# A one-core state-space convolution and MLP kernel: one polar form computed with logarithms and exponentials, table products on POOL, one scratch pool, a new order

## The chip, the cores and the metric

The kernel runs on one core of one Trainium2 chip. A core has five engines with queues of their own: TensorE (PE in the profile, its weight loads PEld), VectorE (DVE), ScalarE (ACT), GpSimd (POOL) and SyncE (SP, which here only issues DMAs). The metric is the device time of one execution in microseconds, lower is better; each kernel is run several times and the median counts.

## What is computed

The reference takes u (1 x 2048 x 512, bfloat16) and computes a state-space convolution with a residual, and then an MLP with a residual:

```python
dt = jnp.exp(log_dt)[:, None]
logdA = dt * (A_re + 1j * A_im)                       # D=512 x N=128
P = jnp.exp(logdA[:, :, None] * l[None, None, :])     # l = 0..L-1, L=2048
K = jnp.einsum("dn,dnl,dn->dl", Cc, P, dt * Bc).real
y = irfft(rfft(pad(u_n)) * rfft(pad(K)))[:L] + u_n * Dskip   # u_n = layernorm(x)
h = x + y
h2 = h + (gelu(layernorm(h) @ w1 + b1) @ w2 + b2)     # 512 -> 1376 -> 512
```

## The kernel before

The program has a front (parameters, tables, first transform, generation of the convolution kernel), a middle (the rest of the transforms and the products in frequency space) and the MLP. The 512 channels are done in two halves of 256 (numbers 0 and 1 in the names below).

*Parameters* (`params`). The coefficient of each state is dt times B times C, a complex number g = (gr, g_i), held as 512 columns on 128 partitions. It is taken to polar form: |g| by a square root, the angle by an arctangent of a half-angle quotient, with a sign s (plus or minus one half) from gr. Tiles w0 to w5 of the pool "w" hold these. The magnitude becomes `amp`; the angle is added to the phase `pc`. The phases are cut into bf16 pieces in `src_p` and `src_q` (parts of M), which TensorE turns into `lps`, and these are copied to PQ0 and PQ1.

*Tables* (`outer`). RP (128 x 1024) and RQ (128 x 640) are outer products of small tables of counts, wp and wq, and of a folded identity m. TensorE multiplies PQ by RP or RQ into `pv` and `qv`, which are phases for all of the powers needed; ScalarE takes their sines (`s`, `sq`).

*Powers.* exp(dt A l) is split into 32 coarse powers (Pt) and 20 fine ones (Q). ScalarE writes the magnitudes with Exp (`exps`), VectorE multiplies Q by amp, and then both by the sines (`p_half`, `q_half`). Each half has 8 products on Pt (of two instructions) and 10 on Q.

*Kernel generation* (`kgen`, L718). For each half, TensorE multiplies Q and Pt in four groups of 256 small matmuls, `kps`; ScalarE copies one part of each to `ku`, VectorE combines both into `samples`. These go to memory (KD_near, KD_far) and come back turned, as `kt`. Groups one and two need the first quarter of the channels, three and four the second.

*First transform* (`norm_in`, L791 to L807). After bn_stats and the roots of the layer norm, sixteen rows of u are normalised (`u`, two buffers), multiplied on TensorE by BD (`aps`), cast to bf16 (`a`, four buffers) and stored by SP to A_dram. Four loads of 1 MB each bring A_dram back as X (L819). `xps` is the next step of that transform, cast into X again.

*Transform tables* (`tables`). M holds the matrices of the transforms, made from sines; the parts `M<-base,Dp` are products of `base` and of `Dp`, which POOL loads out of Dd (L415) after SP has written `ds` there (L400). `R` is copied out of the transposes `rps`.

*Middle* (`conv`). `kfps` is the spectrum of the kernel (from kt), `zps` the first step of the way back; z goes to memory as Zd and comes back turned as ZT, from which TensorE makes the rows `y` and `yh`.

PSUM has three slots "p" that nearly all these tiles share, and one "q".

*The order.* Nothing here is scheduled at run time. Each step is registered as an operation of a list, with the engine or engines that may take it, its rough cost, and the steps it needs. `S.run(ORDER)` then issues the operations in the order of a table of numbers: a number divided by four names the operation, and the rest says which of its engines takes it. Engines then run their queues in that order, and wait on semaphores where an input or a buffer isn't ready.

*Activation tables.* ScalarE's functions lie in sets, and a load (ACT_TABLE_LOAD) stands where the next function isn't in the one that is loaded. In the front before there are loads at the start, for Sqrt (L562), for Sin (L122) and for the second half's Exp (L632).

## Time and profile before

| | before |
|---|---|
| median of 3 runs | 280.96 us |
| lowest, highest | 279.72, 285.02 us |
| the profiled execution's time | 281.15 us |
| its span, first to last instruction | 279.4 us |
| mean granted TensorE clock in the span | 0.901 |
| busy: TensorE, VectorE, ScalarE, POOL | 238.2, 212.5, 173.5, 36.8 us |
| DMA traffic | 31.88 MB, mean 114 GB/s |

The span lies inside the time of the execution; 1.75 us are outside it. Times in the rows are microseconds from the start of the span. A row of the timeline has start, duration, engine, line, operation, output and inputs, a count where rows are put together, and in brackets how long the engine was idle before and what ended that. "issue" stands where the profile shows nothing that was waited for. Rows of one engine overlap by about 0.1 us, so the pace of a chain is taken from start to start.

### The profile page before, as it was taken

How to read it: one execution, taken by the hardware profiler on the slowest of the kernel's cores; microseconds unless marked ns; L12 is line 12 of the kernel's file. 1: busy time of each engine (PE TensorE's matmuls, PEld its weight loads, DVE VectorE, ACT ScalarE, POOL GpSimd, SP SyncE). 2: the span in 40 equal slices, each digit the busy share in tenths (PEclk: the TensorE clock that was granted, in tenths of full speed). 3: DMA queues.
4: the chain of work that ended last, by engine and by line, in shares of the span. 5: the costliest groups of instructions: out<-in, count | busy, mean ns of one | idle time of the engine just before them, and what ended most of it. 6: DMA issues, size and time to landing. Idle time of an engine off the chain costs nothing.

```text
span 279.4 us, 6128 instructions
## 1 busy us (share of the span) xinstructions
PE 238.2 (85%) x2419; PEld 154.9 (55%) x2434; DVE 212.5 (76%) x439; ACT 173.5 (62%) x288; POOL 36.8 (13%) x97
## 2 busy tenths in 40 slices
...
DVE  4999999999973999999669899975672682682012
ACT  4999999999876999997042435215850640630720
...
GB/s 169 263 3 0 38 153 38 158 274 146 124 329 54 146 105 0 37 114 6 5 157 170 236 195 237 264 168 82 322 76 87 31 20 101 33 19 109 25 19 56
DMA packets 41912, 31.88 MB, mean 114 GB/s; under 512 B 14506, under 2 KB 40348, under 8 KB 41628
## 3 DMA queue, kind: packets, MB, share of 16 engines
...
q8 instruction: 19, 0.31, 0.5%
...
## 4 chain that ended last, share of the span: by engine, by line
PE 62%; DVE 19%; ACT 8%; issue 5%; DMA 5%; SPq 0%; DVEq 0%; ACTq 0%; POOLq 0%
PE h1ps L1160 14%; PE o2ps L1172 13%; PE kfps L882 10%; PE kps L718 7%; DVE X L86 4%; DVE st L782 3%; ACT sq L122 3%; PE qv L689 2%; DVE w L74 2%; DMA Zd<-z 1%; DMA ZT<-Zd 1%; DVE Pt L74 1%; PE pv L655 1%; PE y L1119 1%; PE aps L798 1%
## 5 line engine op out<-in xcount | busy, mean ns | idle before, releaser
L1162 ACT ACTIVATE hT<-h1ps,b_sb 128x512 bf16<-128x512 f32 (+3 forms) x55 | 32.4, 601 | 41.2 <-PE h1ps L1160 41.1
L1160 PE MATMUL h1ps<-y2T,wide 128*128 128x512 bf16 (+3 forms) x217 | 40.6, 340 | 0.1
L882 PE MATMUL kfps<-kt,M 128*128 128x256 bf16 x320 | 39.2, 273 | 0.0
L1172 PE MATMUL o2ps<-w_sb,hT 128*128 128x512 bf16 (+3 forms) x183 | 38.5, 366 | 0.2
L74 DVE TENSOR_TENSOR ot<-o2ps,h 128x512 bf16<-128x512 f32 (+1 forms) x17 | 11.0, 658 | 31.1 <-PE o2ps L1172 19.9
L882 PEld LDWEIGHTS <-M 128*128 128x128 bf16 x320 | 31.3, 98 | 5.0 <-issue 1.2
L1160 PEld LDWEIGHTS <-wide 128*128 128x128 bf16 (+1 forms) x220 | 22.3, 102 | 17.1 <-issue 0.6
L1172 PEld LDWEIGHTS <-hT 128*128 128x128 bf16 (+1 forms) x187 | 18.3, 98 | 19.7
L718 PE MATMUL kps<-Q,Pt 128*32 128x20 bf16 x1024 | 18.8, 221 | 6.2 <-issue 6.1
L718 PEld LDWEIGHTS <-Pt 128*32 128x32 bf16 x1024 | 17.9, 169 | 8.6 <-issue 8.6
L625 ACT ACTIVATE Pt<-th 128x256 bf16<-128x256 f32 x64 | 20.8, 404 | 1.6 <-DVE th L74 1.6
L122 ACT ACTIVATE sq<-qv 128x1024 bf16<-128x1024 int16 x20 | 20.6, 1088 | 0.6 <-PE qv L689 0.3
L74 DVE TENSOR_TENSOR Pt<-s,Pt 128x1024 bf16<-128x1024 bf16 x32 | 20.3, 689 | 0.0
L84 ACT CAST z<-zps 128x1024 bf16<-128x1024 f32 (+1 forms) x13 | 12.7, 988 | 11.5 <-PE zps L912 11.1
L122 ACT ACTIVATE s<-pv 128x1024 bf16<-128x1024 int16 x16 | 17.0, 1079 | 0.9 <-PE pv L655 0.6
L415 POOL DMA_DIRECT2D Dp<-Dd x24 | 12.2, 515 | 36.8 <-DMA Dd<-ds 35.6
L632 ACT ACTIVATE Q<-th 128x256 bf16<-128x256 f32 x40 | 13.1, 403 | 4.4 <-PE kps L718 4.4
L798 PE MATMUL aps<-u,BD 128*128 128x512 bf16 x30 | 12.4, 514 | 3.9 <-DVE u L793 1.9
L86 DVE CAST X<-xps 128x1024 bf16<-128x1024 f32 x13 | 15.3, 1212 | 0.0
L84 ACT CAST a<-aps 128x1024 bf16<-128x1024 f32 x14 | 14.4, 1063 | 0.1
L74 DVE TENSOR_TENSOR h<-y,X 128x512 f32<-128x512 f32 (+1 forms) x12 | 9.3, 772 | 6.1 <-PE y L1119 6.1
L339 PE MATMUL v<-crow,three 1*128 1x512 bf16 (+1 forms) x12 | 5.7, 471 | 9.5 <-ACT M L122 7.7
...
## 6 DMA issues: line engine op xcount, KB each, us to landing
...
```

What stands on the lines that cost most here:

```text
L74: nc.vector.tensor_tensor(out, a, b, op)
L84: nc.scalar.copy(out, in_)
L86: nc.vector.tensor_copy(out, in_)
L122: nc.scalar.activation(out, v.bitcast(i16)[..., 0:2 * n:2], ACT.Sin, scale=S2PI / 65536)
L625: nc.scalar.activation(K.Pt[:, k, 1, :], K.th[:, ds], ACT.Exp, scale=float(8 * k))
L632: nc.scalar.activation(K.Q[:, m, 1, :], K.th[:, ds], ACT.Exp, scale=float(OFFS[m]))
L718: nc.tensor.matmul(kps[32 * g:32 * g + 32, i // 8, at:at + 20], lhsT=Pt[:, :, u, c], rhs=Q[:, :, u, c], start=True, stop=True, tile_positi ...
L798: nc.tensor.matmul(ps[:, h, :], lhsT=K.BD[:, h].rearrange("p a b -> p (a b)"), rhs=cell["u"][:], start=True, stop=True)
L882: nc.tensor.matmul(ps[:, k, c, :], lhsT=K.M[:, t, k0 + k, c, :], rhs=kt[:, t, :], start=(c == 1 and t == 0), stop=(t == 4))
L1160: nc.tensor.matmul(pt[:fs, 0:n], lhsT=K.w1_sb[:, dc, fc * P:fc * P + fs], rhs=y2T[tb][:, dc, js, :].rearrange("p a b -> p (a b)"), start=( ...
L1162: nc.scalar.activation(hT[tb % 2][:fs, fc, cols], pt[:fs, 0:n], ACT.Gelu_apprx_tanh, bias=K.b1_sb[:fs, fc:fc + 1], scale=1.0)
L1172: nc.tensor.matmul(pt[:], lhsT=h[:fs, fc, jj * P:(jj + 1) * P], rhs=K.w2_sb[:fs, fc, d], start=(fc == 0), stop=(fc == NFC - 1))
```

## The change

- `params`: Sqrt becomes Ln followed by Exp of half of it; the reciprocal (VectorE, L591) becomes Ln followed by Exp of its negative. A helper `power` does both on ScalarE. The product gr times s becomes an Abs on ScalarE, and s is multiplied into g_i instead, early.
- A helper `logs` loads the set that holds both Ln and Exp ahead of Ln and of all Exp, if another is loaded.
- `outer` is split in three operations (fold, RP, RQ), each of which VectorE or POOL may take. In the new order POOL takes all three.
- The sine tiles, `ku` and w0 to w5 are counted as one pool of six, "w", where there were limits of four (s) and one (ku).
- ORDER is new. It stands for the same list of steps with other numbers. It chooses VectorE for all sixteen u (twelve before), for five casts of a (two before), and for two copies of PQ.

ScalarE from the end of the first half's exponentials, before (w_212 is the squared magnitude, then its root):

```order
21 L562 ACT_TABLE_LOAD
22 L562 ACTIVATE w_212<-w_212 128x512
23 L122 ACT_TABLE_LOAD
24 L122 ACTIVATE wb<-bw 128x2x16
25 L122 ACTIVATE M<-v 128x16x64 x3
26 L522 CAST M<-psw 128x32x16
```

and after (L587 is Ln, L588 the Exp behind it, L591 Abs, L618 the arctangent):

```order
28 L131 ACTIVATE M<-v 128x16x64
29 L124 ACT_TABLE_LOAD
30 L587 ACTIVATE w_213<-w_213 128x512
31 L588 ACTIVATE w_213<-w_213 128x512
32 L650 ACTIVATE Pt<-th 128x256 x6
33 L587 ACTIVATE w_212<-w_210 128x512
34 L588 ACTIVATE w_212<-w_212 128x512
35 L131 ACT_TABLE_LOAD
36 L131 ACTIVATE base_219<-v 128x512
37 L84 CAST a<-aps 128x1024 x3
38 L131 ACTIVATE s<-pv 128x1024
39 L618 ACTIVATE w_212<-w_212 128x512
```

One part of the sines now stands ahead of the load for Ln, six pairs of exponentials stand between the two uses of Ln, and a load for the sines comes behind.

VectorE at the same place, before:

```order
69 L636 TENSOR_TENSOR Q<-Q,amp 128x4x256
70 L74 TENSOR_TENSOR m_177<-ident 128x64
71 L74 TENSOR_TENSOR m_177<-m_177 128x32
72 L74 TENSOR_TENSOR RP<-wp,m_177 128x1024
73 L74 TENSOR_TENSOR m_177<-m_177 128x16
74 L74 TENSOR_TENSOR RQ<-wq,m_177 128x640
75 L116 SCALAR_TENSOR_TENSOR w_209<-w_209,w_212 128x512
76 L519 COPY M<-M 128x16x48 x2
77 L591 RECIPROCAL w_211<-w_209 128x512
78 L74 TENSOR_TENSOR w_211<-w_211,w_210 128x512
79 L116 SCALAR_TENSOR_TENSOR w_211<-w_211,w_213 128x512
```

and after, from the sum that the second Ln reads (w_210):

```order
70 L74 TENSOR_TENSOR w_210<-w_210,w_213 128x512
71 L86 COPY PQ_202<-lps 128x1024
72 L819 TENSOR_SCALAR u<-x,mv,r1y 128x512
73 L74 TENSOR_TENSOR BD<-wb,mask 128x128 x2
74 L86 COPY PQ_201<-lps 128x1024
75 L819 TENSOR_SCALAR u<-x,mv,r1y 128x512
76 L116 SCALAR_TENSOR_TENSOR w_211<-w_211,w_214 128x512
77 L819 TENSOR_SCALAR u<-x,mv,r1y 128x512
78 L74 TENSOR_TENSOR M<-psw,M 128x32x16
79 L68 TENSOR_SCALAR M<-M,cols 128x32x64
80 L819 TENSOR_SCALAR u<-x,mv,r1y 128x512
```

The folds, RP, RQ and the reciprocal are gone from here, and copies of PQ and rows of u stand in their place.

VectorE around the samples of the first half's four kps groups, before:

```order
132 L116 SCALAR_TENSOR_TENSOR samples<-kps,half_sign,ku 128x20x16
133 L74 TENSOR_TENSOR M<-base_218,Dp 128x8x128 x2
134 L74 TENSOR_TENSOR M<-base_218,Dp 128x8x128 x2
135 L74 TENSOR_TENSOR M<-base_217,Dp 128x8x128 x2
136 L116 SCALAR_TENSOR_TENSOR samples<-kps,half_sign,ku 128x20x16
137 L86 COPY R<-rps 128x4x256
138 L74 TENSOR_TENSOR M<-base_217,Dp 128x8x128 x2
139 L74 TENSOR_TENSOR M<-base_219,Dp 128x8x128 x2
140 L116 SCALAR_TENSOR_TENSOR samples<-kps,half_sign,ku 128x20x16
141 L86 CAST X<-xps 128x4x256 x3
```

and after (the last product on Q, and the second to fourth samples):

```order
134 L74 TENSOR_TENSOR Q<-sq,Q 128x32x32
135 L74 TENSOR_TENSOR M<-base_218,Dp 128x8x128 x2
136 L414 TENSOR_REDUCE bf<-nn 128x32 x4
137 L416 CAST bs<-bf 128x128
138 L74 TENSOR_TENSOR M<-base_219,Dp 128x8x128 x2
139 L116 SCALAR_TENSOR_TENSOR samples<-kps,half_sign,ku 128x20x16
140 L74 TENSOR_TENSOR M<-base_220,Dp 128x8x128 x2
141 L116 SCALAR_TENSOR_TENSOR samples<-kps,half_sign,ku 128x20x16
142 L74 TENSOR_TENSOR M<-base_219,Dp 128x8x128 x2
143 L74 TENSOR_TENSOR M<-base_218,Dp 128x8x128 x2
144 L74 TENSOR_TENSOR M<-base_220,Dp 128x8x128 x2
145 L116 SCALAR_TENSOR_TENSOR samples<-kps,half_sign,ku 128x20x16
```

The copy of R and the last two pairs of M products stood between the third and the fourth samples, behind the transposes that follow the fourth group; now all M products stand ahead of the fourth samples, and R behind.

On SP, the write of `ds` (Dd) moves ahead of all stores of `a`, where six stood before it; three X loads are issued in a row ahead of the write of `bs` (Bd), where two were, and the fourth ahead of the first write of the samples, where it stood behind KD_near, M<-Bd and KD_far. Near the end, the residual's second load (512 KB, L1075) and one half of w1 now stand ahead of the last three writes of Zd. On POOL, the folds and RP stand behind the cast of b1, and RQ behind the first four loads of Dp.

The diff, with the table of numbers cut to a line:

```diff
...
 WB = 6
 AT = {"root": 2, "m0": 3, "m1": 3, "bases": 3, "sin0": 3, "exp": (1, 4), "sin": (3, 5)}
 ORDER = [
-    52, 552, 56, 84, 76, 548, 428, 0, 556, 60, 64, 4, 92, 80, 88, 256, 96, 8, 16, 100, 108, 68, 316, 168, 104, 12, 172, 572, 292, 324, 312, 276, 176, 72, 604, 320, 264,
...
+    0, 596, 68, 132, 60, 108, 300, 600, 120, 4, 72, 8, 64, 84, 76, 16, 592, 140, 128, 360, 80, 116, 100, 392, 92, 104, 348, 144, 472, 344, 112, 88, 476, 148, 124, 356,
...
 ]

...

-def tt(nc, out, a, b, op):
-    nc.vector.tensor_tensor(out, a, b, op)
+def tt(nc, out, a, b, op, e="DVE"):
+    (nc.vector if e == "DVE" else nc.gpsimd).tensor_tensor(out, a, b, op)

...
     nc.vector.scalar_tensor_tensor(out, a, s, b, o1, o2)

+NOW = [None]
+
+
+def logs(nc):
+    if NOW[0] != "logs":
+        nc.scalar.preload_act_table_set("natural_log_exp_and_others")
+    NOW[0] = "logs"
+
+
 def sines(nc, out, v):
-
+    NOW[0] = "sines"
     nc.scalar.activation(out, v.bitcast(i16)[..., 0:2 * n:2], ACT.Sin, scale=S2PI / 65536)

...
             count(nc, wq[p0:p1, at:at + cnt], base, pattern + [[0, 2]])
     pl = S.at(10.2)

-    def make():
-        tt(nc, m[:], K.ident[:, 0:64], K.ident[:, 64:128], ALU.add)
-        tt(nc, m[:, 0:32], m[:, 0:32], m[:, 32:64], ALU.add)
-        tt(nc, K.RP[:].rearrange("p i c d -> p (i c) d"), bc(wp[:].rearrange("p i c -> p (i c)").unsqueeze(2), [P, 32, 32]), bc(m[:, 0:32].unsqueeze(1), [P, 32, 32]), ALU.mult)
-        tt(nc, m[:, 32:48], m[:, 0:16], m[:, 16:32], ALU.add)
-        tt(nc, K.RQ[:].rearrange("p i c d -> p (i c) d"), bc(wq[:].rearrange("p i c -> p (i c)").unsqueeze(2), [P, 40, 16]), bc(m[:, 32:48].unsqueeze(1), [P, 40, 16]), ALU.mult)
-
-    K.o_out = S.op("DVE", 2.3, make, [pl])
+    def fold(e):
+        tt(nc, m[:], K.ident[:, 0:64], K.ident[:, 64:128], ALU.add, e)
+        tt(nc, m[:, 0:32], m[:, 0:32], m[:, 32:64], ALU.add, e)
+        tt(nc, m[:, 32:48], m[:, 0:16], m[:, 16:32], ALU.add, e)
+
+    def make_p(e):
+        tt(nc, K.RP[:].rearrange("p i c d -> p (i c) d"), bc(wp[:].rearrange("p i c -> p (i c)").unsqueeze(2), [P, 32, 32]), bc(m[:, 0:32].unsqueeze(1), [P, 32, 32]), ALU.mult, e)
+
+    def make_q(e):
+        tt(nc, K.RQ[:].rearrange("p i c d -> p (i c) d"), bc(wq[:].rearrange("p i c -> p (i c)").unsqueeze(2), [P, 40, 16]), bc(m[:, 32:48].unsqueeze(1), [P, 40, 16]), ALU.mult, e)
+
+    either = ("DVE", "POOL")
+    f = S.op(either, (0.3, 0.4), fold, [pl])
+    K.o_out = [S.op(either, (1.1, 1.3), make_p, [f]), S.op(either, (0.7, 0.9), make_q, [f])]

...
     w = [sc.tile([P, 512], f32, name=f"w{n}", tag="w", bufs=WB) for n in range(6)]
     t, cre, cim = [x[:] for x in w[0:4]], w[4][:], w[5][:]
     pc = sc.tile([P, 512], f32, name="pc", tag="ko", bufs=2)
+    S.group, last = "six", S.group
+    K.o_six = [S.op("NONE", 0.0, lambda: None, acq="w") for _ in range(6)]
+    S.group = last
+    i_gr, i_a, i_gi, i_b, i_re, i_im = K.o_six
     psi0, q0 = psi0[:], q0[:]
     D, A = "DVE", "ACT"
     B = 100
...
         tt(nc, cre, T["cre"], dtb, ALU.mult)
         tt(nc, cim, T["cim"], dtb, ALU.mult)

-    o_c = S2(D, 1.4, cd, [Z["cim"], o_dt], rel=[Z["cre"]], bias=B)
+    o_c = S2(D, 1.4, cd, [Z["cim"], o_dt] + K.o_six, rel=[Z["cre"]], bias=B)
     gr, g_i = t[0], t[2]

     def prod_r():
...
     o_gi = S2(D, 2.1, prod_i, [o_gr], rel=[Z["bre"]], bias=B)

     a, b, m, s = t[1], t[3], cre, cim
-    o_a = S2(A, 0.62, lambda: nc.scalar.activation(a, gr, ACT.Square), [o_gr], bias=B)
+    o_a = S2(A, 0.62, lambda: nc.scalar.activation(a, gr, ACT.Square), [o_gr], rel=[i_gr], bias=B)
     o_b = S2(A, 0.62, lambda: nc.scalar.activation(b, g_i, ACT.Square), [o_gi], bias=B)
     o_m = S2(D, 0.69, lambda: stt(nc, m, a, TINY, b, ALU.max, ALU.add), [o_a, o_b], bias=B)

-    o_q, o_m = o_m, S2(A, 0.62, lambda: nc.scalar.activation(m, m, ACT.Sqrt), [o_m], bias=B, fun=AT["root"])
-
-    def sign():
-        ts(nc, s, gr, 0.0, ALU.is_ge, -0.5, ALU.add)
-        tt(nc, a, gr, s, ALU.mult)
-
-    o_s = S2(D, 1.1, sign, [o_q, o_gi], bias=B)
-    o_d = S2(D, 0.69, lambda: stt(nc, a, a, 2.0, m, ALU.mult, ALU.add), [o_s, o_m], bias=B)
-    K.o_amp = S2(D, 0.69, lambda: stt(nc, K.amp[:], m, 2.0, s, ALU.mult, ALU.mult), [o_s, o_m], bias=B)
-
+    def power(out, v, p):
+        logs(nc)
+        nc.scalar.activation(out, v, ACT.Ln)
+        nc.scalar.activation(out, out, ACT.Exp, scale=p)
+
+    o_q, o_m = o_m, S2(A, 1.05, lambda: power(m, m, 0.5), [o_m], bias=B)
+    o_abs = S2(A, 0.52, lambda: nc.scalar.activation(a, gr, ACT.Abs), [o_q], rel=[i_gr], bias=B)
+    o_s = S2(D, 0.33, lambda: ts(nc, s, gr, 0.0, ALU.is_ge, -0.5, ALU.add), [o_q], rel=[i_gr], bias=B)
+    o_d = S2(D, 0.69, lambda: tt(nc, a, a, m, ALU.add), [o_abs, o_m], rel=[i_re], bias=B)
+    K.o_amp = S2(D, 0.69, lambda: stt(nc, K.amp[:], m, 2.0, s, ALU.mult, ALU.mult), [o_s, o_m], rel=[i_re, i_im], bias=B)
+    o_v = S2(D, 0.69, lambda: stt(nc, g_i, g_i, 2.0, s, ALU.mult, ALU.mult), [o_b, o_s], rel=[i_im], bias=B)

     cell = {}
-    z = S2(A, 0.62, lambda: nc.scalar.copy(grb, gr), [o_gr], bias=B)
+    z = S2(A, 0.62, lambda: nc.scalar.copy(grb, gr), [o_gr], rel=[i_gr], bias=B)

     def k0():
         cell["k"] = psp.tile([1, 512], f32, name="k0", tag="p", bufs=PB)
...

     K.o_top = S2(A, 0.8, top, [z], rel=[z], bias=B)

-    def tangent():
-        nc.vector.reciprocal(b, a)
-        tt(nc, b, b, g_i, ALU.mult)
-        stt(nc, b, b, 2.0, s, ALU.mult, ALU.mult)
-
-    o_t = S2(D, 4.8, tangent, [o_d], bias=B)
-    o_t = S2(A, 0.62, lambda: nc.scalar.activation(b, b, ACT.Arctan), [o_t], bias=B, fun=AT["sin0"])
-    o_arg = S2(D, 0.69, lambda: stt(nc, pc[:], b, 1.0 / math.pi, pc[:], ALU.mult, ALU.add), [o_t, o_pc], bias=B)
+    o_t = S2(A, 1.05, lambda: power(b, a, -1.0), [o_d], rel=[i_a], bias=B)
+    o_t = S2(D, 0.69, lambda: tt(nc, b, b, g_i, ALU.mult), [o_t, o_v], rel=[i_gi], bias=B)
+    def arc():
+        NOW[0] = "sines"
+        nc.scalar.activation(b, b, ACT.Arctan)
+
+    o_t = S2(A, 0.62, arc, [o_t], bias=B, fun=AT["sin0"])
+    o_arg = S2(D, 0.69, lambda: stt(nc, pc[:], b, 1.0 / math.pi, pc[:], ALU.mult, ALU.add), [o_t, o_pc], rel=[i_b], bias=B)
     a5 = S2(A, 0.62, lambda: nc.scalar.copy(into(src_q, 5), as_q(pc[:])), [o_arg], bias=B)
     d5 = S2(D, 0.69, lambda: tt(nc, into(src_q, 6), as_q(pc[:]), into(src_q, 5), ALU.subtract), [a5], bias=B)
     K.o_ql = []
...
     for i in range(16):
         def amp(i=i):
+            logs(nc)
             for k in (15 - i, 16 + i):
                 nc.scalar.activation(K.Pt[:, k, 1, :], K.th[:, ds], ACT.Exp, scale=float(8 * k))

...
     for n in range(5):
         def amp(n=n):
+            logs(nc)
             for m in range(4 * n, 4 * n + 4):
                 nc.scalar.activation(K.Q[:, m, 1, :], K.th[:, ds], ACT.Exp, scale=float(OFFS[m]))

...
                 lo = K.Pt[:, 15::-1, :, dq]
                 tt(nc, lo, s[:], bc(lo[:, :, 1:2, :], [P, 16, 2, 32]), ALU.mult)

-            p = S.op("PE", 0.9, ph, [K.o_pl[hh], K.o_out, K.o_pe[8]], acq="p", bias=-10)
+            p = S.op("PE", 0.9, ph, [K.o_pl[hh], K.o_out[0], K.o_pe[8]], acq="p", bias=-10)
             K.o_phase[hh].append(p)
-            x = S.op("ACT", 0.94, sn, [p] + K.o_pe, acq="s", rel=[p], fun=AT["sin"][hh])
+            x = S.op("ACT", 0.94, sn, [p] + K.o_pe + K.o_six, acq="w", rel=[p], fun=AT["sin"][hh])
             K.o_p[qd].append(S.op("DVE", 1.23, mul, [x] + K.o_pe, rel=[x]))

...
                 o = K.Q[:, m0:m1, :, dq]
                 tt(nc, o, cell["s"][:], bc(o[:, :, 1:2, :], [P, m1 - m0, 2, nd]), ALU.mult)

-            x = S.op("PE", 0.9, ph, [K.o_ql[hh], K.o_out, K.o_pe[8]], acq="p")
+            x = S.op("PE", 0.9, ph, [K.o_ql[hh], K.o_out[1], K.o_pe[8]], acq="p")
             K.o_phase[hh].append(x)
-            z = S.op("ACT", 0.94, sn, [x] + K.o_qe, acq="s", rel=[x], fun=AT["sin"][hh])
+            z = S.op("ACT", 0.94, sn, [x] + K.o_qe + K.o_six, acq="w", rel=[x], fun=AT["sin"][hh])
             K.o_q[qd].append(S.op("DVE", 0.63, mul, [z] + K.o_qe, rel=[z]))

...

             m = S.op("PE", 2.6, mms, K.o_p[s] + K.o_q[s], acq="p")
-            r = S.op("ACT", 0.45, real, [m] + ends, acq="ku")
+            r = S.op("ACT", 0.45, real, [m] + ends, acq="w")
             ends.append(S.op("DVE", 0.5, out, [r], rel=[m, r], acq="ko" if not s and not hv else None))
...
     early = ExitStack()
     xq, c2, lp = (early.enter_context(tc.tile_pool(name=nm, bufs=1, side="right")) for nm in ("xq", "c2", "lp"))
+    NOW[0] = None
+    logs(nc)
...
         xp = ctx.enter_context(tc.tile_pool(name="xp", bufs=1, side="right"))
         K.X = xp.tile([P, 16, 2, 512], bf16, name="X")

-    S = Sched({"p": PB, "q": QB, "kf": 3, "F0": 1, "F1": 1, "F2": 1, "B": 1, "z": 3, "pa": 2, "s": 4, "ko": 2, "ku": 1, "u": 2, "a": 4, "kt": 2})
+    S = Sched({"p": PB, "q": QB, "kf": 3, "F0": 1, "F1": 1, "F2": 1, "B": 1, "z": 3, "pa": 2, "w": 6, "ko": 2, "u": 2, "a": 4, "kt": 2})
```

5 lines of the change are left out of this document (4 added, 1 removed), and 38 rows, old and new, of the table ORDER.

## Prediction

> **What bounds the kernel now.** I read the page's shares, its forty slices and its chain first, then the busy table by stage, then the waits of the engine that carries each stage. From the page:
>
> ```profile
> PE 238.2 (85%) x2419; PEld 154.9 (55%) x2434; DVE 212.5 (76%) x439; ACT 173.5 (62%) x288; POOL 36.8 (13%) x97
> DVE  4999999999973999999669899975672682682012
> ACT  4999999999876999997042435215850640630720
> PE 62%; DVE 19%; ACT 8%; issue 5%; DMA 5%; SPq 0%; DVEq 0%; ACTq 0%; POOLq 0%
> ```
>
> The shares mix two kernels. Until about slice 10 (70 us) VectorE and ScalarE are both full; from slice 19 on TensorE is. The table by stage (start:end, length, then busy time of each engine, granted clock, DMA share, GB/s) gives the border:
>
> ```profile
> 30.00:70.00 40.00, 33.07 (x196) 13.71 (x202) 39.33 (x79) 39.88 (x49) 12.20 (x24) 0.75 0.44 141
> 70.00:75.00 5.00, 4.95 (x210) 4.31 (x210) 4.80 (x9) 4.03 (x5) 0.00 (x0) 1.00 0.26 73
> 75.00:86.00 11.00, 4.91 (x284) 4.71 (x282) 7.29 (x16) 6.95 (x6) 0.00 (x0) 0.60 0.92 286
> 86.00:106.00 20.00, 17.75 (x158) 13.87 (x156) 17.98 (x22) 18.39 (x55) 1.58 (x2) 0.88 0.36 89
> 106.00:130.00 24.00, 22.27 (x382) 16.37 (x383) 23.89 (x41) 21.71 (x23) 0.89 (x1) 1.00 0.16 45
> 130.00:180.00 50.00, 49.96 (x676) 44.62 (x676) 42.89 (x73) 19.07 (x22) 8.27 (x10) 1.00 0.62 169
> ```
>
> From 30 to 70 VectorE idles 0.67 of 40 us and ScalarE 0.12: both bound it. From 75 to 86 no engine is full, and the DMA share is 0.92. After that TensorE idles 2.25 us (86 to 106), 1.73 (106 to 130) and 0.04 (130 to 180). So what the change is worth is read at one point: the end of the last kernel-generation group (kps) of the first half, and the TensorE idle time behind it. That point, and what holds it up:
>
> ```profile
> PE kps L718 <- issue: 6.1, 2, 4.1
> ```
>
> ```profile
> 69.14 2.32 PE L718 MATMUL kps<-Q,Pt 128*32 128x20 bf16 x128
> 73.26 2.45 PE L718 MATMUL kps<-Q,Pt 128*32 128x20 bf16 x134
> 77.66 2.33 PE L718 MATMUL kps<-Q,Pt 128*32 128x20 bf16 x128 [1.95 <-issue]
> 84.13 2.25 PE L718 MATMUL kps<-Q,Pt 128*32 128x20 bf16 x122 [4.14 <-issue]
> ```
>
> ```profile
> 69.07 0.51 SPq L807 DMA_DIRECT2D A_dram<-a  x1
> 73.54 1.00 SPq L819 DMA_DIRECT2D X<-A_dram  x2
> 77.14 2.81 SPq L819 DMA_DIRECT2D X<-A_dram  x1
> q8 instruction: 19, 0.31, 0.5%
> ```
>
> The fourth group ends at 84.13 + 2.25 = 86.4 us. Two of the four waited 6.1 us for no semaphore, and both stand in the time in which three 1 MB loads of X hold the DMA engines. The last row is the queue that brings 0.31 MB of instructions through the same engines. My reading, which these rows suggest but don't prove, is that TensorE's instructions came late.
>
> **The change, part by part.** All against the profiled execution: span 279.4, time 281.15 us, so 1.75 around the span, and 0.19 above the median of 280.96.
>
> *VectorE, front.*
>
> ```profile
> 37.83 0.18 DVE L74 TENSOR_TENSOR m<-ident 128x64 bf16<-128x64 bf16 x1
> 40.48 0.69 DVE L116 SCALAR_TENSOR_TENSOR w<-w,w 128x512 f32<-128x512 f32 x1
> 41.62 3.34 DVE L591 RECIPROCAL w<-w 128x512 f32<-128x512 f32 x1
> 88.02 0.69 DVE L86 COPY R<-rps 128x1024 bf16<-128x1024 bf16 x1 [5.69 <-PE rps L443]
> 88.62 2.49 DVE L74 TENSOR_TENSOR M<-base,Dp 128x1024 bf16<-128x1024 bf16 x4
> 91.03 0.54 DVE L116 SCALAR_TENSOR_TENSOR samples<-kps,half_sign,ku 128x320 bf16<-128x320 f32 x1
> 91.49 3.47 DVE L86 CAST X<-xps 128x1024 bf16<-128x1024 f32 x3
> 36.30 0.41 DVE L793 TENSOR_SCALAR u<-x,mv,r1y 128x512 bf16<-128x512 bf16 x1
> ```
>
> Off it go the tables' products with their folds (start to start, 40.48 - 37.83 = 2.65), the reciprocal (3.34), and one 512-wide product, which I price at 0.6 (0.69 in the row of its like, less the 0.09 by which rows overlap, as 88.62 - 88.02 = 0.60 against 0.69 shows): 6.6 us. But the new order chooses VectorE for work that ScalarE did: four u (0.41 - 0.09 = 0.32 each, 1.3), two 1024-wide copies of PQ (as the R copy, 0.60 each, 1.2) and three casts of a, like the X casts at 3.47/3 = 1.15 each, 3.4: 5.9 us back. Net -0.7 us. So the engine that bounds the front is hardly relieved. A wait comes in at its start: the product nf now stands before the first bn_stats and needs POOL's lf counts, the end of which I put at 7.56 us from the row
>
> ```profile
> 7.03 0.53 POOL L166 IOTA lf<- 128x2 f32 x5
> ```
>
> where VectorE would by my count of the rows ahead be ready about 0.9 us sooner. -0.7 + 0.9: the front's last products end where they did (+0.2, taken as 0).
>
> *ScalarE, front.*
>
> ```profile
> 24.79 1.28 ACT L562 ACT_TABLE_LOAD   x1
> 26.09 0.63 ACT L562 ACTIVATE w<-w 128x512 f32<-128x512 f32 x1
> 38.79 0.81 ACT L791 ACTIVATE u<-x,mv,r1y 128x512 bf16<-128x512 bf16 x1
> 39.50 0.37 ACT L91 ACTIVATE Dm<-dps 128x256 bf16<-128x256 bf16 x1
> 34.95 3.94 ACT L84 CAST a<-aps 128x1024 bf16<-128x1024 f32 x4
> 40.47 1.92 ACT L84 COPY PQ<-lps 128x1024 bf16<-128x1024 bf16 x2
> ```
>
> Added: Ln, Exp, Ln, Exp and Abs for one Sqrt, four more at 0.6 = +2.4, and one more table load, 26.09 - 24.79 = +1.3. No Ln or Abs stands in the trace; they are bounded by the narrowest 512-wide ACTIVATE at 0.6 and the widest I see at twice that (+4.9), and I take the Sqrt's. Moved off: four u (39.50 - 38.79 = 0.7 each) -2.8, three casts (3.94/4) -3.0, the two copies -1.9. Net +3.7 - 7.7 = -4.0 us. ScalarE gets slack; VectorE stays full, so this is worth nothing by itself, and it covers the chain's own waits (the second Ln waits for VectorE's sum). If that cover went, the cost would be the one or two us of that wait.
>
> [...]
>
> *POOL.* It takes folds, RP and RQ.
>
> ```profile
> 16.09 0.19 POOL L1058 CAST b_sb<-b_bf 128x11 f32<-128x11 bf16 x1 [2.80 <-DMA b_bf<-in_B_b_dram]
> 51.93 6.06 POOL L415 DMA_DIRECT2D Dp<-Dd  x11 [35.65 <-DMA Dd<-ds]
> L166 POOL IOTA si<- 1x128 bf16 x6 | 3.4, 588 | 0.0
> ```
>
> No two-input product runs on POOL in this trace. Below: VectorE's 2.65 us. Above: the slowest POOL rate per element in the rows, 588/128 = 4.6 ns, over 1024 + 640 elements, 7.6 us. RP stands behind the cast at 16.09, and its first reader pv behind the copies of PQ, which come after the norm's sums, well past 30 us. RQ stands behind four Dp issues (0.55 each by 6.06/11), which wait for Dd, and Dd's write now goes ahead of all A_dram stores on SP. POOL idles 35.65 us here, so both ends are hidden: 0. With the cover gone it would cost POOL's time on pv.
>
> [...]
>
> *The point at 86.4.* The first kps group starts when VectorE has made the last product of its quarter. Before, nine products of 0.6 and one samples (0.47) stood between that product and the end of the last Q product, 5.9 us; now eleven and one samples, 7.1 us. That last product ends at
>
> ```profile
> 73.65 1.51 DVE L74 TENSOR_TENSOR Q<-sq,Q 128x1024 bf16<-128x1024 bf16 x2
> 75.07 1.26 DVE L395 TENSOR_REDUCE bf<-nn 128x32 f32<-128x64 f32 x4
> ```
>
> 75.07, and by the front's sum still does; so the first group starts 1.2 us earlier, at 68.0. The second follows it when ScalarE has read it (ku) and made one sq, about 0.4 + 1.0 us behind its end at 70.3, at 71.7 where it was 73.26. The X loads move from 73.54 to about 71 as well: the last casts of a now end about 66.5 by VectorE's sum, and before, the loads came 4.5 us behind the last store (69.07). So groups two to four stand under the loads as before, and I keep their time, 86.4 - 73.3 = 13.1 us: 71.7 + 13.1 = 84.8, -1.6 us. Bounds: no stall, 86.4 - 6.1 = 80.3; and 88, if the second group stalls 3 us too, as the other two did on average.
>
> *Behind it.* Both programs issue the same matmuls behind the fourth group, so the end moves with that point and with TensorE's idle time only. Before, VectorE made R, four M products (2.49 us) and the samples (91.03) between the end of kps and the first X cast at 91.49. Now all M products stand ahead of the fourth samples, in the time of the stall (9.6 us of work from 75.1, to about 85), and the samples come right behind the group. Of the 2.25 us idle (86 to 106) I take 1.5 as gone; bounds: none, and all 3.98 up to 130. Late next are the second half's exponentials: their table load now stands behind the fourth ku (1.3 us, and ScalarE has 1.6 us idle in 86 to 106).
>
> *Tail.*
>
> ```profile
> 183.73 0.39 PE L969 MATMUL yh<-ZT,Dm 96*128 96x256 bf16 x2 [2.13 <-DMA ZT<-Zd]
> ```
>
> SP now issues 512 KB of residual and a w1 half ahead of the last three Zd writes, whose landing this wait is. They go out when an earlier write has landed, some us before the last casts, so I set 0; bounds -1 to +2.
>
> The scratch pool as one changes only which tiles are counted together, with no buffer fewer: 0.
>
> **Sum.** 0 (front) - 1.6 (kps) - 1.5 (idle) + 0 (tail) = -3.1: 281.15 - 3.1 = 278.05, say 278.0 us, 1.1% under the median.
>
> **Rivals.**
> (A) The stall goes away, because groups and loads part. Then kps ends at 80.3, -6.1, and the idle time makes it -7.6; but VectorE's M products hold the fourth samples, and with them a PSUM slot, until about 85: that gives back 1 to 2.5 us, so 274.5 to 276.0. For it: the stall needs the loads. Against: both move by the same 2 us or so.
> (C) The stall grows to its upper bound: 88 - 86.4 - 1.5 = +0.1, 281.3; with the tail's +2, 283.3. For it: a second group nearer the loads' start.
> (D) POOL's products slow VectorE: if it ran at half speed during POOL's upper bound of 7.6 us, +3.8 - 3.1, so 281.9. No row shows such a thing. [...]
> (B) Slower than before: all sixteen u now stand in VectorE's queue, with two buffers, so each waits for a matmul two back, which waits for one of three PSUM slots that ScalarE's casts free. Where this ring is late, VectorE, with 0.67 us of idle in 40 before, stops with all its products behind it. At 0.7 us for each of the last 13 u it costs 9.1 us: 281.15 + 9.1 - 3.1 = 287.2. It decides from about 0.7 each. Against it: the twelve u that it has already show no such wait in the stage from 30 to 70.
>
> **Chances.** Two per cent of 280.96, 5.6 us, is about what a measurement of this kernel tells from no change: the borders are 275.3 and 286.6. Forecast 0.39 (own range 275.3 to 281); A 0.33, two thirds of it under 275.3, since a stall that goes leaves the loads' end earlier too; C and D 0.10; B 0.18, all of it over 286.6. Faster 0.22, same 0.60, slower 0.18. The range takes in all but A's lowest part and B up to its price: 273 to 287.
>
> **What would show it.** Right: no RECIPROCAL on VectorE, VectorE still full from 30 to 70; "issue" waits at kps of about 6 us with the last group ending at 85; samples within 1 us of it; under 0.5 us of idle on TensorE from there to the first kfps. Wrong: kps ending before 82.5 (A) or after 87 (C); VectorE waits for aps in the front (B); VectorE's 512-wide products over 0.8 us while POOL multiplies (D); more than 3 us at yh for ZT.

## The result and the profile after

The changed kernel is slower: median 286.25 us (282.89 to 290.45, 20 runs) against 281.96 us (278.96 to 285.19, 20 runs) for the kernel before on the same chip, a ratio of 1.0135 with a 95% interval of 1.0097 to 1.0173. Some executions of either kernel fall in a slower state, and the ratios here leave these out, so they are not the quotients of the medians. The forecast was 278.0 us, 1.1% faster. So the sign was wrong; the size stays inside the 2% that the forecast called "same" and inside its range. The profiled execution after took 283.9 us, with a span of 282.1 (before: 279.4).

Milestones of the profiled executions, in us from the start of the span. "Both repairs" is the kernel that the experiments ended with (e8_w1_early below).

| point | before | forecast | after | both repairs |
|---|---|---|---|---|
| first kps group of half 0 starts | 69.14 | 68.0 | 70.36 | 68.08 |
| its last kps group ends | 86.38 | 84.8 | 87.89 | 85.55 |
| kps of half 1 end | 140.11 | | 140.25 | 138.18 |
| last kfps ends | 177.34 | | 182.18 | 176.06 |
| yh ends | 189.92 | | 193.50 | 187.77 |
| first h1ps on y2T | 195.19 | | 198.27 | 192.29 |
| span | 279.4 | 276.3 | 282.1 | 276.1 |

The column shows two losses: 1.2 to 1.5 us in the front, where 1.1 to 1.6 were to be won, and some 4.7 us between 140 and 182, a stretch for which the forecast had no term. Between them the time falls back to that of before, as the forecast's idle term said. The stages of the page after, in the same columns as before (start:end, length, busy time of PE, PEld, DVE, ACT, POOL, granted clock, DMA share, GB/s):

```profile
30.00:70.00 40.00, 26.42 (x139) 11.62 (x139) 39.48 (x91) 38.40 (x50) 13.56 (x25) 0.82 0.45 135
75.00:86.00 11.00, 4.64 (x254) 4.34 (x254) 9.58 (x20) 5.58 (x5) 0.00 (x0) 0.65 1.09 343
86.00:106.00 20.00, 19.01 (x254) 15.76 (x248) 17.74 (x22) 17.27 (x51) 1.61 (x2) 0.85 0.19 46
106.00:130.00 24.00, 22.23 (x381) 16.27 (x384) 23.90 (x41) 23.12 (x29) 0.00 (x0) 1.00 0.05 12
130.00:180.00 50.00, 47.42 (x635) 41.08 (x634) 35.96 (x60) 19.75 (x23) 9.14 (x11) 0.97 0.59 152
```

VectorE is as full from 30 to 70 as before (39.48 of 40). ScalarE has the slack that was forecast (38.40 where it had 39.88). From 86 to 106 TensorE idles 0.99 us, where it idled 2.25. From 130 to 180 it idles 2.58, where it idled 0.04: that is new.

*The first loss.* Both engines of the front in order of time; the last bracket of a row, where there is one, is the idle time before it:

```profile
17.22 0.69 DVE L74 TENSOR_TENSOR w<-w,w 128x512 f32<-128x512 f32 x1
...
17.95 1.90 POOL L74 TENSOR_TENSOR RP<-wp,m 128x1024 bf16<-128x1024 bf16 x1
...
18.43 1.70 DVE L68 TENSOR_SCALAR psw<-psi 128x512 f32<-128x512 f32 x1
...
38.02 1.98 DVE L819 TENSOR_SCALAR u<-x,mv,r1y 128x512 bf16<-128x512 bf16 x1
...
38.56 1.28 POOL L74 TENSOR_TENSOR RQ<-wq,m 128x640 bf16<-128x640 bf16 x1
```

A TENSOR_SCALAR of 512 columns takes 0.41 us (36.30 in the rows of before). Here one takes 1.70 and one 1.98, and each ends 0.2 to 0.3 us behind the POOL product beside it (18.43 + 1.70 = 20.13 against 17.95 + 1.90 = 19.85; 40.00 against 39.84). VectorE shows no idle time here: its rows are longer instead. 1.29 + 1.57 = 2.9 us are lost, 0.2 more than the 2.65 us of products that POOL took over. One detail does not fit a plain hold: this u starts 0.54 us ahead of the row of RQ, beside four DMA issues of POOL (36.32 to 38.54), and such issues held no u elsewhere (0.40 at 40.93).

```profile
76.32 0.68 DVE L74 TENSOR_TENSOR Q<-sq,Q 128x1024 bf16<-128x1024 bf16 x1
```

So the last Q product of the half ends at 77.00 instead of 75.07. TensorE's groups behind it, and the loads of X on SP:

```profile
70.36 2.32 PE L744 MATMUL kps<-Q,Pt 128*32 128x20 bf16 x128
74.33 2.39 PE L744 MATMUL kps<-Q,Pt 128*32 128x20 bf16 x131 [0.22 <-ACT sq L131]
77.05 0.25 PE L744 MATMUL kps<-Q,Pt 128*32 128x20 bf16 x4 [0.33 <-DVE Q L74]
81.10 2.32 PE L744 MATMUL kps<-Q,Pt 128*32 128x20 bf16 x128 [3.79 <-issue]
85.65 2.24 PE L744 MATMUL kps<-Q,Pt 128*32 128x20 bf16 x121 [2.23 <-issue]
```

```profile
72.03 2.38 SPq L845 DMA_DIRECT2D X<-A_dram  x3
...
80.02 1.62 SPq L845 DMA_DIRECT2D X<-A_dram  x1
```

The stall is what the forecast kept, 3.79 + 2.23 = 6.0 us under the same loads.

*The second loss.* SP from 141 to 143 before the change:

```profile
141.25 0.33 SPq L747 DMA_DIRECT2D KD_near<-samples  x1
...
143.03 0.36 SPq L753 DMA_DIRECT2D kt<-KD_near  x1
```

SP between 140 and 152 after it, and what TensorE waits for there:

```profile
140.28 0.56 SPq L959 DMA_DIRECT2D ZT<-Zd  x1
141.33 0.35 SPq L773 DMA_DIRECT2D KD_near<-samples  x1
...
145.71 0.38 SPq L779 DMA_DIRECT2D kt<-KD_near  x1
146.15 0.48 SPq L1101 DMA_DIRECT2D X<-in_A_u_dram  x1
146.68 0.58 SPq L779 DMA_DIRECT2D kt<-KD_near  x1
147.30 4.54 SPq L779 DMA_DIRECT2D kt<-KD_far  x3
```

```profile
151.04 0.27 PE L908 MATMUL kfps<-kt,M 128*128 128x256 bf16 x1 [0.54 <-DMA kt<-KD_near]
153.07 0.27 PE L908 MATMUL kfps<-kt,M 128*128 128x256 bf16 x1 [1.76 <-DMA kt<-KD_near]
153.57 1.98 PE L908 MATMUL kfps<-kt,M 128*128 128x256 bf16 x8 [0.23 <-DMA kt<-KD_far]
...
187.31 0.38 PE L995 MATMUL yh<-ZT,Dm 96*128 96x256 bf16 x2 [0.75 <-DMA ZT<-Zd]
```

The write of KD_near goes out at the time of before (141.25), but the first load of kt, which reads it, comes 4.4 us later where it came 1.8 us later (143.03), with a read of ZT on SP and one on POOL now ahead of it; and the 512 KB of residual stands between the two near loads of kt. (e1_kt_first below, with these behind kt, has the 1.8 us again.) TensorE waits 0.54 + 1.76 + 0.23 = 2.5 us for kt, where it waited for none. Another 1.7 us of the 4.7 is a stretch right behind at a granted clock down to 0.50 (last section); before, one that cost as much stood between 193 and 197 (0.58, 0.50, 0.50 and 0.72 in four stretches of 1 us), so it moved and is no difference between the two. At yh, the one place of this stretch that the forecast looked at, the wait has shrunk from 2.13 to 0.75 us: TensorE now comes late enough to find ZT there.

### The profile page after: what moved, and what is told of

It is laid out like the page before. It is cut to its first block, busy times and chain, and to the rows that moved or that the text cites. A ratio compares the mean times of both kernels' runs of the same rounds, so it can differ in the third digit from the quotient of the medians.

```text
span 282.1 us, 6122 instructions
## 1 busy us (share of the span) xinstructions
PE 236.1 (84%) x2418; PEld 155.3 (55%) x2434; DVE 211.7 (75%) x438; ACT 172.2 (61%) x287; POOL 41.2 (15%) x102
## 4 chain that ended last, share of the span: by engine, by line
PE 50%; DVE 29%; issue 7%; DMA 6%; ACT 3%; POOL 2%; SPq 2%; DVEq 0%; POOLq 0%
PE h1ps L1186 13%; PE o2ps L1198 13%; PE kfps L908 9%; PE kps L744 5%; DVE st L808 3%; DVE X L86 3%; DVE Pt L74 3%; DVE u L819 2%; DVE w L74 2%; DVE Q L74 2%; DVE Q L662 2%; SPq L779 1%; DMA KD_near<-samples 1%; DVE a L86 1%; DMA ZT<-Zd 1%
## 5 line engine op out<-in xcount | busy, mean ns | idle before, releaser
L908 PE MATMUL kfps<-kt,M 128*128 128x256 bf16 x320 | 41.0, 278 | 2.5 <-DMA kt<-KD_near 2.3
L1186 PE MATMUL h1ps<-y2T,wide 128*128 128x512 bf16 (+3 forms) x217 | 39.9, 336 | 0.2
L908 PEld LDWEIGHTS <-M 128*128 128x128 bf16 x320 | 31.9, 100 | 8.2 <-issue 3.7
L824 PE MATMUL aps<-u,BD 128*128 128x512 bf16 x30 | 9.8, 421 | 10.7 <-DVE BD L74 6.2
L84 ACT CAST kf<-kfps 128x1024 bf16<-128x1024 f32 (+1 forms) x8 | 7.7, 963 | 16.3 <-PE kfps L908 16.3
L86 DVE CAST X<-xps 128x1024 bf16<-128x1024 f32 x12 | 14.2, 1217 | 1.4 <-PE xps L865 1.4
L959 POOL DMA_DIRECT2D ZT<-Zd x6 | 3.0, 508 | 83.1 <-ACT ku L748 46.6
L74 DVE TENSOR_TENSOR Q<-sq,Q 128x1024 bf16<-128x1024 bf16 x20 | 13.2, 683 | 0.0
```

The lines of the kernel that those rows point to most:

```text
L74: (nc.vector if e == "DVE" else nc.gpsimd).tensor_tensor(out, a, b, op)
L84: nc.scalar.copy(out, in_)
L86: nc.vector.tensor_copy(out, in_)
L824: nc.tensor.matmul(ps[:, h, :], lhsT=K.BD[:, h].rearrange("p a b -> p (a b)"), rhs=cell["u"][:], start=True, stop=True)
L908: nc.tensor.matmul(ps[:, k, c, :], lhsT=K.M[:, t, k0 + k, c, :], rhs=kt[:, t, :], start=(c == 1 and t == 0), stop=(t == 4))
L1186: nc.tensor.matmul(pt[:fs, 0:n], lhsT=K.w1_sb[:, dc, fc * P:fc * P + fs], rhs=y2T[tb][:, dc, js, :].rearrange("p a b -> p (a b)"), start=( ...
```

## The experiments

Two theories were put up from these rows. P: POOL's products hold VectorE. K: the order of the loads in the second half starves TensorE of kt. In the diffs, rows name an instruction of the order with its line; only the order is edited unless a line of code is shown. Ratios are to the kernel before on the same chip at the same time.

**e1_kt_first: the loads of kt ahead of ZT, residual and w1 half.** On SP (POOL loses its ZT and w1 row to SP):

```diff
-L959 DMA ZT<-Zd_69 16x8192
 L773 DMA KD_near_68<-samples 128x512
...
-L779 DMA kt<-KD_near_68 128x4x64
+L779 DMA kt<-KD_near_68 128x4x64 x2
+L779 DMA kt<-KD_far_67 128x4x64 x3
 L1101 DMA X<-in_A_u_dram 128x8x256
-L779 DMA kt<-KD_near_68 128x4x64
-L779 DMA kt<-KD_far_67 128x4x64 x3
+L959 DMA ZT<-Zd_69 16x8192
```

> The changed kernel with one edit in the order: two ZT loads, the second load of the residual and the first half of w1 are issued behind the second half's kt loads on SP instead of ahead of or between them. Theory K (those loads, about 1.4 MB, stand on the DMA engines ahead of KD_near and kt): TensorE's 2.5 us of waits for kt near 151 us vanish, the granted clock at 152 to 158 stays at 1.0 instead of 0.73 and 0.71, the last kfps comes about 4 us earlier (181.9 to about 178), and the span falls by 2 to 4 us from 282.1. Rival O (TensorE merely reaches these kfps sooner in the new order, and kt is as late as before): the waits stay at 2 us or more, and the span within 1 us.

Measured: 285.11 us, 1.0121 (1.0078 to 1.0165); span 283.3. No wait for kt is left, the first load of kt goes out 1.8 us behind the write of KD_near again (144.89 and 143.09), and the last kfps ends at 179.89, 2.3 us earlier, where 4 were expected. From the end of the second half's kps (142.00, where the changed kernel has 140.25) it is 4.0 us less. The time did not fall by the 2 to 4 us expected. Further on:

```profile
186.78 0.38 PE L995 MATMUL yh<-ZT,Dm 96*128 96x256 bf16 x2 [2.23 <-DMA ZT<-Zd]
196.28 1.86 PE L1034 MATMUL y<-ZT,Dm 128*128 128x256 bf16 x8 [3.32 <-DMA ZT<-Zd]
```

The wait for kt was real, and taking it away alone moved it to ZT. TensorE now reaches the last reads of ZT too early, and the residual and w1 half (182.60 and 183.31 on SP) still stand between them and the last writes of Zd.

**e2_outer_early: folds, RP and RQ on POOL ahead of the bias loads.**

```diff
 L496 MEMSET M 128x32x16
+L74 TENSOR_TENSOR m_178<-ident 128x64
+L74 TENSOR_TENSOR m_178<-m_178 128x32
+L74 TENSOR_TENSOR m_178<-m_178 128x16
+L74 TENSOR_TENSOR RP<-wp,m_178 128x1024
+L74 TENSOR_TENSOR RQ<-wq,m_178 128x640
 L1079 MEMSET b_bf 128x11
```

> The changed kernel with one edit in the order: POOL makes the folds, RP and RQ ahead of the bias loads, at about 11 to 15.5 us, where VectorE's queue holds tensor_tensor and bn_stats rows but no 512-wide tensor_scalar. Theory P (a VectorE tensor_scalar that comes while POOL multiplies two inputs waits for POOL to finish): the rows psw<-psi and the first u<-x go from 1.70 and 1.98 us to 0.4 each, VectorE's last Q product of the first half comes 2.5 to 2.9 us sooner than 77.0, the first kps about 2.5 us sooner than 70.4; how much of it reaches the end depends on the instruction stalls and kt. Rival W (those two rows are long for another reason, such as a wait that the profile does not show): they stay near 1.7 and 2.0.

Measured: 282.95 us, 1.0047 (1.0015 to 1.008). In order of time:

```profile
12.39 1.90 POOL L74 TENSOR_TENSOR RP<-wp,m 128x1024 bf16<-128x1024 bf16 x1
12.77 0.67 DVE L808 BATCH_NORM_STATS2 st<-x 128x6 f32<-128x512 bf16 x1
13.37 1.26 DVE L74 TENSOR_TENSOR w<-tps_bre,w 128x512 f32<-128x512 f32 x2
14.24 1.26 POOL L74 TENSOR_TENSOR RQ<-wq,m 128x640 bf16<-128x640 bf16 x1
14.66 1.39 DVE L74 TENSOR_TENSOR w<-w,w 128x512 f32<-128x512 f32 x1
...
19.09 0.41 DVE L68 TENSOR_SCALAR psw<-psi 128x512 f32<-128x512 f32 x1
...
38.72 0.40 DVE L819 TENSOR_SCALAR u<-x,mv,r1y 128x512 bf16<-128x512 bf16 x1
```

psw and u are back at 0.41 and 0.40, and the first kps starts at 68.16: within 0.2 us of the forecast's 68.0. Theory P holds, and its rival, that the two rows are long for another reason, is out. The ratio is 0.9 points under the changed kernel's 1.0135, with intervals apart, though the two were not measured side by side. The rows also sort the instructions: beside the same POOL products a product with one input in PSUM (tps_bre) and the statistics keep their times (1.26 for two, 0.67), while a product of two SBUF tiles takes 1.39 instead of 0.69.

**e3_outer_dve: the same five instructions on VectorE, at the places where the change had them.** In the order each of the three steps takes VectorE for POOL; no other row moves.

> The changed kernel with the choice of engine alone undone: folds, RP and RQ on VectorE, at the same places of the order. Theory P: psw and the first u fall to 0.4 us each (-2.9 us on VectorE), and the products cost it 2.65 us again, so the first kps stays within 0.5 us of 70.4 and the span within 1 us of 282.1: the move to POOL gained nothing. Rival W: the two rows stay long and VectorE is 2.65 us later, first kps near 73, span about 2 us more.

Measured: 283.22 us, 1.0062 (1.002 to 1.0105); first kps at 69.75.

```profile
18.86 0.41 DVE L68 TENSOR_SCALAR psw<-psi 128x512 f32<-128x512 f32 x1
29.98 1.21 DVE L74 TENSOR_TENSOR RP<-wp,m 128x1024 bf16<-128x1024 bf16 x1
```

VectorE does the work itself, and the first kps still comes 0.6 us earlier than with POOL's help at those places (70.28 to 71.12 in four profiled executions with POOL's products there; within 0.5 of 70.4 was expected). The move to POOL was a loss where it stood. Between e2 and e3 the first kps differs by 1.6 us and the ratio by 0.0015, well inside the intervals: with the loads as they were, the gain at the first kps did not show at the end.

**e4_both: e1 and e2 together.**

> Both edits of the order together, kt loads first and POOL's products early. Theories K and P together: the first kps near 67.9, no wait for kt, clock 1.0 at 152 to 158, span 276 to 279, faster than the changed kernel by 1 to 2% and near or below the kernel before (279.4). If the stall of 6 us at kps grows by what the front gains, the span stays at 278 to 280, and only K's part is kept.

Measured: 282.41 us, 1.0051 (1.0015 to 1.0086), no better than e2 alone; the span is 280.0, where 276 to 279 were expected.

```profile
182.83 0.38 PE L995 MATMUL yh<-ZT,Dm 96*128 96x256 bf16 x2 [2.27 <-DMA ZT<-Zd]
```

The last kfps ends at 176.0, 1.3 us earlier than before the change, but yh ends 0.8 us later than it did; a granted clock of 0.60 from 183 to 186 and 0.87 from 186 to 190 costs it 1.7 us, so the end of yh says little here, the wait more. The residual and the w1 half go out at 178.60 and 179.31, right behind the last reads of ZT.

**e5_tail: e4 with these two loads moved.**

```diff
 L961 DMA Zd_69<-z 128x4x256
+L1101 DMA X<-in_A_u_dram 128x8x256
 L979 DMA wide<-Ds 4x8x128 x4
...
+L1075 DMA wide<-in_B_w_dram 128x2x768
 L959 DMA ZT<-Zd_70 16x8192 x3
-L1101 DMA X<-in_A_u_dram 128x8x256
-L1075 DMA wide<-in_B_w_dram 128x2x768
```

> The order of e4_both, with the second residual load put ahead of the eight reads of ZT and the w1 half behind the last of the first three writes of Zd that follow them, instead of both right behind the reads. If the 2.3 us that yh waited for ZT in e4_both came from these 512 KB and the w1 half sharing the DMA engines with the reads (theory K2), the wait at the first yh falls under 0.7 us, the end of yh comes from 190.7 to about 188.5, and the profiled span from 280.0 to 277 to 278.5: a ratio of 0.990 to 1.000 against the kernel before. Rival T: the wait for ZT is the time of the last write of Zd and the read behind it, whoever else uses the DMA engines: then the wait stays near 2 us, the end of yh at 190 to 191 and the ratio at 1.003 to 1.006.

Measured: 282.33 us, 0.9955 (0.9908 to 1.0002); the wait at yh is 1.9 us. As the diff shows, the w1 half still went out (176.40) ahead of the last three reads of ZT (178.77), so this run did not decide between its theories.

**e8_w1_early: e5 with that w1 half on POOL, ahead of the strided loads of wide.**

```diff
 L969 MEMSET wide 128x4096
+L1075 DMA wide<-in_B_w_dram 128x2x768
 L979 DMA wide<-Ds 4x8x128 x4
```

> e5_tail with the second w1 half right behind the first, on POOL, so that none of the three 384 to 512 KB loads stands among the last writes of Zd and reads of ZT, as none did before the change. In e5_tail the w1 half went out at 176.40, still ahead of the last three reads of ZT (178.77), so that run did not decide between K2 and T. K2 (the loads delay the reads): the wait at the first yh falls from 1.9 to under 0.7 us, yh ends at or before 189, span 276.5 to 278.5, ratio 0.985 to 0.993. T (the round trip of the last writes and reads of Zd sets yh, as the 2.13 us there in the kernel before already was): the wait stays at 1.5 to 2.5 us, yh ends at 190 to 192, span 279 to 281, ratio 0.994 to 1.002.

Measured: 280.27 us, 0.9931 (0.9885 to 0.9978); span 276.1.

```profile
181.59 0.38 PE L995 MATMUL yh<-ZT,Dm 96*128 96x256 bf16 x2 [1.14 <-DMA Zd<-z]
```

The ratio stands at the border of the two theories, and its interval covers parts of both. The wait of 1.14 us lies between them too, and it was 1.7 in the repeat below. What is shown is the step from e4: its ratio of 1.0051 falls to 0.9931 with intervals apart, so the places of these loads cost something, by runs on two chips. How much of the wait that is left belongs to the round trip of Zd and ZT stays open.

**The table of four: e10_loads_only (e8 without its POOL edit), e11_both_again (e8 once more) and e12_after_again (the changed kernel once more), on one chip.**

> e8_w1_early without its POOL edit: the folds, RP and RQ stand on POOL where the change put them, the loads of the second half as in e8_w1_early. With e2_outer_early (POOL edit alone), e8_w1_early (both) and the changed kernel (neither) this makes a table of four. If the two losses are separate and add up (theory S2), this is 0.9% (the POOL edit's 2.5 us) longer than e8_w1_early and 1.2% shorter than the changed kernel: a ratio of 1.000 to 1.004 against the kernel before, no wait for kt, and psw and one u held as before (1.70 and 1.98 us). Rival: the loads' order is worth something only when the front ends early; then the ratio stays at 1.008 to 1.013, as in e1_kt_first.

> e8_w1_early once more, beside e10_loads_only and the changed kernel on one chip. Expected by the first run: a ratio of 0.989 to 0.998 against the kernel before, 0.975 to 0.985 against the changed kernel. If the first run's gain was the scatter of half-rate stretches of TensorE's clock (it had none between 140 and 200), the ratio comes back to 1.000.

> The changed kernel itself, unedited, on the same chip as e10_loads_only and e11_both_again, so that the three can be compared in one session: 1.010 to 1.017 against the kernel before.

| ratio to before | products as changed | products early |
|---|---|---|
| loads as changed | e12: 1.0181 (1.0112 to 1.025) | e2, on another chip: 1.0047 (1.0015 to 1.008) |
| loads repaired | e10: 1.0001 (0.9955 to 1.0047) | e11: 0.994 (0.9897 to 0.9982) |

e10 has no wait for kt left and keeps a u of 1.98 us. Its psw came 2 us later, at 20.50, and took 0.40; the instruction that met RP instead was a product of two SBUF tiles, held for 0.83 us (1.52 against 0.69):

```profile
17.52 1.90 POOL L74 TENSOR_TENSOR RP<-wp,m 128x1024 bf16<-128x1024 bf16 x1
...
18.45 1.52 DVE L74 TENSOR_TENSOR w<-w,w 128x512 f32<-128x512 f32 x1
```

So a hold needs no particular instruction, only one of these kinds at that moment. The changed kernel itself came out 1.8% slower beside these two, its interval reaching past the expected 1.010 to 1.017. By this chip the loads are worth 1.8 points (1.0181 to 1.0001), with intervals apart, and the POOL edit another 0.6, less than the 0.9 expected and with intervals that overlap. The other way round, over two chips, it is 1.3 for POOL and 1.1 for the loads. The two add up within their intervals, and which is the larger stays open. Nor need all of the loads' part be a loss by the change: at yh the repaired order waits 1.14 and 1.71 us, less than the 2.13 of before. With both repaired the changed kernel is 0.6 to 0.7% under the kernel before, twice, on two chips (0.9931, 0.994), and its ratio to itself as it was is 0.994/1.0181 = 0.976.

**e7_reciprocal: e2 with the reciprocal back on VectorE.**

```diff
-    o_t = S2(A, 1.05, lambda: power(b, a, -1.0), [o_d], rel=[i_a], bias=B)
+    o_t = S2(D, 3.4, lambda: nc.vector.reciprocal(b, a), [o_d], rel=[i_a], bias=B)
```

> The order of e2_outer_early, with the reciprocal of the coefficients taken back from ScalarE's logarithm and exponential to one VectorE reciprocal, as before the change. If VectorE sets the front (theory V, on which the prediction's sum stood), the first kps comes 2.6 to 3.4 us later than e2's 68.2, at 70.8 to 71.6, and the span is 1 to 3 us longer than e2's. Rival: ScalarE's added pair of operations lies on the path too, and taking it off returns about as much: the first kps stays within 0.7 us of 68.2.

Measured: 285.57 us, 1.0129 (1.0049 to 1.021).

```profile
39.02 3.34 DVE L614 RECIPROCAL w<-w 128x512 f32<-128x512 f32 x1
```

The first kps starts at 71.33, 3.2 us behind e2. VectorE is the bound of the front, and at the first kps the exponential in place of the reciprocal is worth what the reciprocal's row says. At the end the two runs are 0.8 points apart, on two chips, with intervals that overlap.

**e9_quarters: RP and RQ on POOL as four instructions of a quarter each, at the places of the change.**

```diff
-        tt(nc, K.RP[:].rearrange("p i c d -> p (i c) d"), bc(wp[:].rearrange("p i c -> p (i c)").unsqueeze(2), [P, 32, 32]), bc(m[:, 0:32].unsqueeze(1), [P, 32, 32]), ALU.mult, e)
+        [tt(nc, K.RP[:].rearrange("p i c d -> p (i c) d")[:, 8 * i:8 * i + 8], bc(wp[:].rearrange("p i c -> p (i c)")[:, 8 * i:8 * i + 8].unsqueeze(2), [P, 8, 32]), bc(m[:, 0:32].unsqueeze(1), [P, 8, 32]), ALU.mult, e) for i in range(4)]
```

> The changed kernel with POOL's products RP and RQ each written as four instructions of a quarter, at the same places. Theory L (a VectorE instruction of that kind waits for the end of the POOL instruction that runs, and no longer): psw falls from 1.70 to 0.6 to 1.1 us and the slow u from 1.98 to 0.6 to 0.9, since only one quarter (about 0.5 us for RP, 0.35 for RQ) is waited for, and the first kps comes 1 to 2 us earlier than 70.36. Theory S (VectorE runs slowed by a factor of about 4 as long as POOL has work queued): they stay over 1.4 and 1.6 us and the first kps at 70 or later.

Measured, one run: 286.94 us, span 285.1, first kps at 69.64. VectorE's rows and then POOL's:

```profile
18.38 0.41 DVE L68 TENSOR_SCALAR psw<-psi 128x512 f32<-128x512 f32 x1
18.83 0.72 DVE L70 TENSOR_SCALAR q<-psw 128x512 f32<-128x512 f32 x1
19.58 0.98 DVE L74 TENSOR_TENSOR psw<-psw,q 128x512 f32<-128x512 f32 x1
...
37.27 0.68 DVE L819 TENSOR_SCALAR u<-x,mv,r1y 128x512 bf16<-128x512 bf16 x1
```

```profile
17.90 3.13 POOL L74 TENSOR_TENSOR RP<-wp,m 128x256 bf16<-128x256 bf16 x4
37.80 1.81 POOL L74 TENSOR_TENSOR RQ<-wq,m 128x160 bf16<-128x160 bf16 x4
```

No VectorE instruction loses more than 0.3 us now (0.72 against 0.43, 0.98 against 0.69, 0.68 against 0.40), though POOL works for 3.13 us where it worked for 1.90. That is theory L: an instruction of this kind waits for the POOL instruction that runs, not for POOL's queue. POOL's own growth suggests that it waits for VectorE in turn (its two later folds take 0.88 us in the changed kernel, 0.54 in e2); no run tested that. The first kps came only 0.7 us earlier than 70.36, where 1 to 2 were expected. VectorE loses some 1.4 us here (0.9 in these rows and 0.54 in two of BD, 1.02 against 0.48) where it lost 2.9, so of 1.5 us saved 0.7 came out; why not more was not followed up.

**e6_x_late: e2 with the loads of X behind the write of the samples.** On SP:

```diff
-L845 DMA X<-A_dram 128x8x512 x3
+L773 DMA KD_near_66<-samples 128x512
+L845 DMA X<-A_dram 128x8x512 x4
```

> The order of e2_outer_early, with the four loads of X issued on SP behind the first write of the samples, which waits for the eighth samples of kgen0 (about 80 us), instead of at 72. Theory F: TensorE's 6 us of waits named issue at the kps matmuls belong to the time in which these loads hold the DMA engines; then they fall to under 1 us in all before the loads, the last kps of the first half ends at 80 to 82 instead of 85.7, and the stall, if it is tied to the loads, comes back behind them at the xps matmuls or is replaced by a wait for X of 2 to 4 us there. Rival: the stall belongs to the place in TensorE's program (the first run of those instructions) and stays at 6 us at kps; then the end of kps stays at 85 to 86 and the wait for X is added, span 284 to 287.

Measured: 294.94 us, 1.0432 (1.0358 to 1.0506); the kps of half 0 end at 82.05.

```profile
76.08 2.32 PE L744 MATMUL kps<-Q,Pt 128*32 128x20 bf16 x128 [0.90 <-issue]
79.81 2.24 PE L744 MATMUL kps<-Q,Pt 128*32 128x20 bf16 x121 [1.41 <-issue]
...
92.21 0.37 PE L862 MATMUL xps<-X,M 128*128 128x256 bf16 x1 [8.38 <-DMA X<-A_dram]
```

Without the loads the stall falls from 6.0 us (4.10 + 1.95 in e2) to 2.3, not under 1; in eight other profiled executions (before, after, e2, and e8 to e12) it lies between 5.9 and 7.3. So some 3.7 us of it belong to the loads and 2.3 to something that is there with the DMA engines idle (share 0.02 from 75 to 82). As an edit it costs far more than it gives, since X is then waited for (13.9 us in all).

## Why the prediction was wrong, step by step

- **"POOL ... both ends are hidden: 0": failed.** The step priced POOL's time on POOL and asked only whether POOL was idle and its readers late. Both were so: 1.90 and 1.28 us, 3.2 in all, inside the bounds of 2.65 to 7.6. The cost fell on VectorE, 2.9 us, more than the 2.65 taken off it. Rival D named a slowing of VectorE by POOL's products, and priced it at a half speed over 7.6 us, 3.8 us, at a chance of 0.10 with C. Its sign, 512-wide products over 0.8 us while POOL multiplies, came true. The half speed was the forecast's assumption, and no run shows it: in its place the runs showed a hold until the POOL instruction ends, for some kinds of instruction. Held were TENSOR_SCALARs of 512 columns (1.70 and 1.98 us for 0.41) and products of two SBUF tiles (1.39 in e2 and 1.52 in e10 for 0.69); products with one input in PSUM and the statistics were not (1.26 for two and 0.67 in e2). What the held kinds have in common no run shows.
- **VectorE's front, "taken as 0": right but for that.** With POOL's products out of the way (e2) the first kps starts at 68.16 against a forecast of 68.0. That the two are so near is luck in part: e2 still loses 0.7 us to a hold, and the wait for lf, set at 0.9 us, did not come (nf starts at 8.18 without idle time, lf ends at 7.57). The reciprocal's term (3.34) measured 3.2 at the first kps (e7).
- **ScalarE's slack: right.** Ln, Exp and Abs took 0.63 us each, as the Sqrt did, and up to 70 ScalarE was busy 3.7 us less (1.5 of it from 30 on), where 4.0 were forecast. That this slack alone is worth nothing was not tested.
- **"I keep their time" (the stall of 6.1 us): right in size, 6.0.** Rivals A and C are out: the last group did end past 87 (87.89), the sign given for C, but because the groups started late and not by a longer stall. The prediction read the stall as TensorE's instructions coming late under the loads, a reading that its rows "suggest but don't prove". e6 shows that the loads cause 3.7 of the 6.0 us; that it is the instructions that wait for them stays unproven.
- **Idle behind kps, -1.5: right, -1.26** (2.25 to 0.99).
- **"The end moves with that point and with TensorE's idle time only", and then "Tail ... 0": failed.** The rule held, and the forecast did not apply it behind 130: it read one wait there (yh for ZT) and not the order of SP's and POOL's loads between 140 and 150, where the change had put ZT, residual and the w1 half around the loads of kt. The term that it put at nothing was 2.5 us of waits for kt and, with the loads behind them, 1.8% of the time (e12 to e10). It was the same kind of reading that the forecast did make for the last Zd writes: a queue row, its bytes, and who waits for what stands behind it.
- **Rival B (the ring of u): out.** In the front TensorE waits for VectorE's BD and u (6.2 and 1.3 us), not VectorE for aps; from 30 to 70 VectorE idles 0.52 us.

In sum, two terms put at nothing turned a gain into a loss. With both repaired the kernel stands 0.7 and 0.6% under the kernel before (0.9931, 0.994), some 1.9 and 1.7 us, where the forecast had 3.1; single spans scatter from 1.0 to 3.3 us under it (278.4 and 276.1 against 279.4). So the gain was put too high as well: 0.75 us of that stand at the last kps of the first half (85.55 against 84.8), and the rest was not followed up. That the measured time lies inside 273 to 287 is luck: the upper end came from rival B, which is out.
